# Column sums of the second weights moved from GpSimd to VectorE, from the fourth block on

## The chip, the cores and the metric

One core of a Trainium2 chip runs the kernel. TensorE (PE) multiplies matrices, VectorE (DVE) and ScalarE (ACT) work on elements, GpSimd (POOL) does a little of the same, and SyncE (SP) starts all transfers of data. Each engine runs its own queue in order and waits on semaphores where it needs another's result. The metric is the device time of one execution in microseconds (us).

## The reference, cut

Windowed attention over 4 batches, 8 heads, 576 positions, followed by two feed-forward layers on 2304 tokens:

```python
attn = softmax(where(0 <= i - j < 128, scale * q @ k.T - slope * |i - j|, -1e9)) @ v
x    = attn.transpose(0, 2, 1, 3).reshape(2304, 512)
h    = maximum(x @ w_in1, 0)
x    = (s * h * h + b) @ w_out1            # 512 -> 2048 -> 512
h    = maximum(x @ w_in2, 0)
out  = (h * h) @ w_out2
```

The first layer's `b` adds the same row to every token: `b` times the column sums of `w_out1`. The kernel adds that row afterwards, and so it needs those column sums.

## The kernel before

Every float32 number that TensorE multiplies is split into a high half and a low half in the format fp32r, and a product takes three matmuls (high by high, high by low, low by high). `split` makes the halves: ScalarE copies the high one (L99), VectorE subtracts to get the low one (L102). The weights come as 64-bit words and are made into float32 by `convert`, a chain over three engines for each part `st` of 128x1024 or 128x512: ScalarE L119, VectorE L120, ScalarE L121, VectorE L122, GpSimd L123 (an integer add), and then the split into `wih`/`wil` (first weights) or `woh`/`wol` (second weights). Layer 1 has four groups of weights (0 to 3); a group is 4 of the 16 slices of 128 hidden units.

The tokens go in blocks of 256 (`b`, `u`), nine in all with the one of tails. Attention of a block is made in four pairs of heads (`pair_unit`): scores `s` on PE, masked maximum on VectorE (L186), exponentials on ScalarE (L190), sums and reciprocals `nd` (L193, L194), scaling of the probabilities `pr` (L268), transposes `t` on PE (L270), output `u` on PE (L281), and the split of the output into `xh` and `xl`. In block (0, 1) the probabilities and their transposes lie in weight tiles that aren't needed yet and are named `f_`.

`mlp` runs the first layer over a block: for each slice `f` PE makes `ha` (12 matmuls, L357) in one of two PSUM buffers, ScalarE takes the ReLU and VectorE the square `ra` (L367, L368), the split gives `ga`, and two slices later PE multiplies `ga` with the second weights into `oa` (12 matmuls, L394). So a buffer of `ha` comes free with the `ra` of VectorE two slices on. The lambdas in `behind` (loads, conversions, attention pieces of later blocks, sums) are traced between the slices; a scheduler then orders each engine's queue by its own estimate of the times, with `issue_after` as an added edge of order on one engine.

The first three blocks are done in halves while the weights are still being converted (`half` over groups 0 and 1, `other` over groups 2 and 3, whose names are `hc`, `rc`, `gc`, `oc`). Blocks 3 to 6 then run over all slices, and behind them stand the tails' attention, the next blocks' attention and the column sums: `sum_rows` adds four slices' worth of `woh` and `wol`, 128x512 each, into `csum`, 32 additions in all. They are traced from block 3 on, but on GpSimd nothing holds them there: the scheduler puts them as early as their weights exist. `csum` is read once, by the matmuls of `sum_column` (L544) during the last block of layer 1.

Of the kernel before, what the change touches and what calls it, by code (L numbers as in the profile page):

```python
# [8 lines left out]
F32 = mybir.dt.float32  # L9
# [4 lines left out]
ALU = mybir.AluOpType  # L14
# [5 lines left out]
def attention_mlp2_kernel(ctx, tc, first0, first1, qkv0, qkv1, qkvt, w_in1, w_out1, s_in, b_in, w_in2, w_out2, out):  # L20
# [7 lines left out]
    nc = tc.nc  # L28
# [9 lines left out]
    BLK = 256  # L38
# [28 lines left out]
    csum = const.tile([P, DM], F32, tag="csum", name="csum")  # L67
# [23 lines left out]
    def split(hi, lo, src, copy, sub):  # L91
        copy(hi, src)
        sub(lo, src, hi.bitcast(F32))
# [4 lines left out]
    def act_copy(o, i):  # L98
        return nc.scalar.activation(o, i, AF.Copy)  # L99

    def dve_sub(o, a, b_):
        nc.vector.tensor_tensor(o, a, b_, ALU.subtract)  # L102


    n_g = [0]

    marks = []

    def convert(words, hi, lo):

        l32, h32 = words[..., 0], words[..., 1]
        with tc.issue_after(marks[-4]) if len(marks) > 3 else nullcontext():
            nc.scalar.activation(l32, l32.bitcast(U32), AF.Copy, scale=2.0 ** -29)  # L119
        nc.vector.scalar_tensor_tensor(l32, h32, -2 ** 31, l32, ALU.bitwise_and, ALU.bitwise_or)  # L120
        nc.scalar.activation(h32.bitcast(F32), h32.bitcast(F32), AF.Copy, scale=2.0 ** -112)  # L121
        nc.vector.tensor_scalar(h32, h32, 3, None, ALU.logical_shift_left)  # L122
        nc.gpsimd.tensor_tensor(l32, h32, l32, ALU.add)  # L123
        split(hi, lo, l32.bitcast(F32), act_copy, dve_sub)
# [73 lines left out]
    def pair_unit(b, u, hp):  # L198
# [3 lines left out]
        early = b == 0  # L202
# [5 lines left out]
        def probabilities():  # L208
# [25 lines left out]
            if early:  # L234
                passes = [(qr, kr)]
            else:
                nqk = BLK + nj * P
                qk = ap.tile([P, 2, BLK + 3 * P], F32R, tag="qk", name=f"qk{nm}", bufs=1)
                split(qk[:, 0, :nqk], qk[:, 1, :nqk], raw[:, :nqk], act_copy, dve_sub)
                (qh, kh), (ql, kl) = [(qk[:, y, :BLK], qk[:, y, BLK:nqk]) for y in range(2)]  # L240
                passes = [(qh, kh), (qh, kl), (ql, kh)]
# [13 lines left out]
        def outputs():  # L255
# [17 lines left out]
            up = ps.tile([P, 3 * P], F32, tag="u", name=f"u{nm}", bufs=1) if hp % 2 or u or not early else psum("o", f"u{nm}")  # L273

            with tc.issue_after(moved.ins):
                k = 0
                for i, (ka, ncol) in enumerate(tiles):
                    nk = ncol // P
                    for j in range(nk):
# [3 lines left out]
                                             skip_group_check=True)  # L283
                        k += 1
            xh, xl = xt[(b, u)]
            split(xh[:, hp, :], xl[:, hp, :], up[:, :BLK], act_copy if early and u else act_mark, dve_sub)
        return [probabilities, outputs]

    def first_pair(u, hp):
# [147 lines left out]
    wts1, wts2 = [], []  # L437
    pools = {"ps": ps}

    def psum(tag, name):  # L440
        return pools["ps"].tile([P, DM], F32, tag=tag, name=name)
# [56 lines left out]
    nc.sync.dma_start(b_sb, b_in.partition_broadcast(P))  # L498
    def sum_rows(g, j):

        for w in (wts1[g][2], wts1[g][3]):
            nc.gpsimd.tensor_tensor(csum, csum, w[:, j, :].bitcast(F32), ALU.add)

    nc.gpsimd.memset(csum, 0.0)
    sums = [lambda g=g, j=j: sum_rows(g, j) for g in range(NG) for j in range(GF)]
    tails = [[lambda b=b, hp=hp: tail_unit(b, hp) for hp in range(H // 2)] for b in range(B)]
    for i in range(NHALF, LAST - 1):
# [117 lines left out]
```

## Time and profile before

| | us |
|---|---|
| median of 3 runs | 1009.8 (1008.94 to 1010.32) |
| the profiled execution | 1010.16 |
| its span, first to last instruction | 1008.4 |
| PE busy | 974.3 (97%) |
| VectorE busy | 522.2 (52%) |
| ScalarE busy | 490.2 (49%) |
| GpSimd busy | 130.4 (13%) |
| the 32 additions on GpSimd, first start to last start | 38.0 to 167.1 |

A busy share is a mean over stages that differ: VectorE is nearly always at work in the first 170 us, in which weights are converted, and about half of the time after it. A busy PE is not PE at its peak, since its clock is granted in two levels, 1.2 and 2.4 GHz, shown as 0.5 and 1.0.

### The profile page before, as it was taken

The numbers are of one execution on the slowest core, as the hardware profiler recorded it, in microseconds if no ns is written. First come the engines' busy times: TensorE is split into PE (matmuls) and PEld (weight loads), VectorE is DVE, ScalarE is ACT, GpSimd is POOL, SyncE is SP. The second block draws the span as 40 slices with busy tenths as digits, with TensorE's granted clock in tenths as the row PEclk, the third lists the DMA queues.
The fourth block names the chain that finished last, engine by engine and source line by source line (L and its number), as shares of the span: only waits on it lengthen the run. The fifth ranks groups of instructions, "written<-read, shape, count | busy, mean of one in ns | idle before, by whom it ended". The sixth has DMA issues, their size and how long they took to land.

```text
span 1008.4 us, 16815 instructions
## 1 busy us (share of the span) xinstructions
PE 974.3 (97%) x6504; PEld 854.1 (85%) x6504; DVE 522.2 (52%) x1236; ACT 490.2 (49%) x1157; POOL 130.4 (13%) x118
## 2 busy tenths in 40 slices
PE   6899889999999999999999899999999999999997
PEld 4689778999989999899999888778888888898886
DVE  6997998443564444544265787754223222432222
ACT  7977766454555445554355666664222312322221
POOL 4653655000000000000010312310000000000000
PEclk9799989999999999999999999999999999999999
DMA  8135423111221211211052444422000100100001
GB/s 333 43 129 167 162 88 106 53 53 35 60 67 46 72 34 52 75 54 39 9 184 74 131 173 147 147 83 74 11 1 5 59 1 0 43 1 22 1 1 42
DMA packets 46928, 72.39 MB, mean 72 GB/s; under 512 B 6656, under 2 KB 27136, under 8 KB 46848
## 3 DMA queue, kind: packets, MB, share of 16 engines
q1 hardware_dynamic: 46848, 71.32, 21.8%
q8 instruction: 51, 0.84, 0.3%
q14 instruction: 29, 0.24, 0.1%
HBM read 59.77 MB, written 11.53 MB: 71 GB/s over the span
## 4 chain that ended last, share of the span: by engine, by line
PE 75%; DVE 9%; DMA 9%; ACT 4%; issue 2%; SPq 0%; POOL 0%; ACTq 0%; DVEq 0%; POOLq 0%
PE ob L403 15%; PE hb L357 14%; PE ha L357 13%; PE oa L394 13%; DMA st<-w_in 4%; PE oc L394 3%; PE s L245 3%; PE hc L357 3%; PE u L281 3%; DMA st<-w_out 2%; PE hbtail L357 2%; PE t L270 2%; PE obtail L403 2%; DVE wol L102 1%; DVE wil L102 1%
## 5 line engine op out<-in xcount | busy, mean ns | idle before, releaser
L394 PE MATMUL oa<-ga,woh 128*128 128x256 f32 x960 | 189.6, 289 | 7.3 <-ACT ga L99 3.9
L403 PE MATMUL ob<-woh,gb 128*128 128x512 f32 x512 | 168.9, 391 | 1.4 <-ACT gb L99 1.3
L394 PEld LDWEIGHTS oa<-ga,woh 128*128 128x128 f32 x960 | 152.2, 192 | 14.0 <-DVE ga L102 5.2
L394 PE MATMUL oa<-ga,wol 128*128 128x256 f32 x480 | 135.6, 286 | 0.1
L368 DVE SCALAR_TENSOR_TENSOR rb<-hb,rb 128x512 f32<-128x512 f32 x64 | 44.1, 690 | 147.4 <-ACT rb L367 147.2
L403 PEld LDWEIGHTS ob<-woh,gb 128*128 128x128 f32 x512 | 95.9, 188 | 23.8 <-ACT gb L99 3.3
L367 ACT ACTIVATE rb<-hb 128x512 f32<-128x512 f32 x64 | 38.2, 597 | 156.5 <-PE hb L357 152.0
L123 POOL TENSOR_TENSOR st<-st 128x512 int32<-128x512 int32 (+1 forms) x50 | 70.3, 1407 | 235.1 <-DVE st L122 177.4
L403 PE MATMUL ob<-wol,gb 128*128 128x512 f32 x256 | 99.7, 389 | 0.0
L394 PEld LDWEIGHTS oa<-ga,wol 128*128 128x128 f32 x480 | 92.2, 192 | 1.2 <-issue 0.9
L368 DVE SCALAR_TENSOR_TENSOR ra<-ha,ra 128x256 f32<-128x256 f32 x120 | 50.0, 419 | 62.9 <-ACT ra L367 62.4
L102 DVE TENSOR_TENSOR ga<-ra,ga 128x256 fp32r<-128x256 f32 x120 | 65.8, 552 | 29.0 <-ACT ga L99 28.4
L99 ACT ACTIVATE ga<-ra 128x256 fp32r<-128x256 f32 x120 | 49.5, 416 | 42.4 <-DVE ra L368 41.7
L102 DVE TENSOR_TENSOR gb<-rb,gb 128x512 fp32r<-128x512 f32 x64 | 45.5, 711 | 44.0 <-ACT gb L99 43.8
L367 ACT ACTIVATE ra<-ha 128x256 f32<-128x256 f32 x120 | 45.0, 378 | 43.6 <-PE ha L357 39.0
L99 ACT ACTIVATE gb<-rb 128x512 fp32r<-128x512 f32 x64 | 40.4, 632 | 47.7 <-DVE rb L368 35.6
L120 DVE SCALAR_TENSOR_TENSOR st<-st 128x512 int32<-128x512 int32 (+1 forms) x50 | 47.3, 950 | 26.3 <-ACT st L119 25.8
L119 ACT ACTIVATE st<-st 128x512 int32<-128x512 uint32 (+1 forms) x50 | 40.5, 814 | 35.2 <-DMA st<-w_out 19.3
L403 PEld LDWEIGHTS ob<-wol,gb 128*128 128x128 f32 x256 | 48.1, 188 | 9.7
L190 ACT ACTIVATE pr<-pr,nd 128x256 f32<-128x256 f32 (+1 forms) x96 | 45.1, 473 | 3.8 <-DVE nd L186 3.4
L121 ACT ACTIVATE st<-st 128x512 f32<-128x512 f32 (+1 forms) x50 | 40.5, 813 | 7.0 <-DVE st L120 7.0
L186 DVE CUSTOM_DVE_ANT_0 pr<-s,bases 128x256 f32<-128x256 f32 (+1 forms) x96 | 32.1, 386 | 19.4 <-PE t L270 15.0
(204 smaller groups left out, 2387.1 us busy)
## 6 DMA issues: line engine op xcount, KB each, us to landing
st<-w_out SPq DMA_DIRECT2D x20, 512.0 KB, 3.9
st<-w_in SPq DMA_DIRECT2D x8, 1024.0 KB, 6.8
st<-w_in SPq DMA_DIRECT2D x16, 512.0 KB, 4.8
st<-w_out SPq DMA_DIRECT2D x6, 1024.0 KB, 8.9
raw<-qkv SPq DMA_DIRECT2D x36, 128.0 KB, 2.6
xib<-acc SPq DMA_DIRECT2D x9, 512.0 KB, 4.4
out<-obb SPq DMA_DIRECT2D x16, 256.0 KB, 2.0
raw<-qkv SPq DMA_DIRECT2D x24, 160.0 KB, 2.9
```

What stands on the lines that cost most here:

```text
L99: return nc.scalar.activation(o, i, AF.Copy)
L102: nc.vector.tensor_tensor(o, a, b_, ALU.subtract)
L119: nc.scalar.activation(l32, l32.bitcast(U32), AF.Copy, scale=2.0 ** -29)
L120: nc.vector.scalar_tensor_tensor(l32, h32, -2 ** 31, l32, ALU.bitwise_and, ALU.bitwise_or)
L121: nc.scalar.activation(h32.bitcast(F32), h32.bitcast(F32), AF.Copy, scale=2.0 ** -112)
L123: nc.gpsimd.tensor_tensor(l32, h32, l32, ALU.add)
L190: nc.scalar.activation(pr, pr, AF.Exp, bias=nmx, scale=-1.0, accum_out=den)
L357: nc.tensor.matmul(ph, w_[:, cc, j * P:(j + 1) * P], x_[:, cc, :], start=(k == 0), stop=(k == 3 * NCC - 1))
L367: nc.scalar.activation(r, ph, AF.Relu)
L368: nc.vector.scalar_tensor_tensor(r, ph, 0.0, r, ALU.max, ALU.mult)
L394: nc.tensor.matmul(po[o // 2][:, (o % 2) * BLK:(o % 2 + 1) * BLK], w_[:, j, o * P:(o + 1) * P], g[:, gi, :], start=(start and n == 0 and o ...
L403: nc.tensor.matmul(po[t], g[:, gi, t * P:(t + 1) * P], w_[:, j, :], start=(start and n == 0), stop=(stop and n == 2))
```

## The change

`sum_rows` adds on VectorE instead of GpSimd, inside an `issue_after` on `lows[-1]`, the last low half of an attention output that was traced before it. `lows` is filled by `dve_mark`, which does what `dve_sub` does and keeps the instruction. Nothing else is edited; `csum` is still cleared by GpSimd.

```diff
+    def dve_mark(o, a, b_):
+        lows.append(nc.vector.tensor_tensor(o, a, b_, ALU.subtract).ins)
...
+    lows = []
...
-            split(xh[:, hp, :], xl[:, hp, :], up[:, :BLK], act_copy if early and u else act_mark, dve_sub)
+            split(xh[:, hp, :], xl[:, hp, :], up[:, :BLK], act_copy if early and u else act_mark, dve_mark)
...
     def sum_rows(g, j):
 
-        for w in (wts1[g][2], wts1[g][3]):
-            nc.gpsimd.tensor_tensor(csum, csum, w[:, j, :].bitcast(F32), ALU.add)
+        with tc.issue_after(lows[-1]):
+            for w in (wts1[g][2], wts1[g][3]):
+                nc.vector.tensor_tensor(csum, csum, w[:, j, :].bitcast(F32), ALU.add)
```

The diff adds four lines ahead of the kernel's body, so L102 of before is L102 (`dve_mark`) or L105 (`dve_sub`) of the change, L268 is L272, L368 is L372, and so on. Three places show what it moves.

GpSimd from the conversion of the last part of group 0 on, before; `st03` is part 3 of group 0, and `woh0`, `wol0` are the second weights of group 0:

```order
L123 TENSOR_TENSOR st03_326<-st03_326 128x1024
L502 TENSOR_TENSOR csum_90<-csum_90,woh0_317 128x512
L502 TENSOR_TENSOR csum_90<-csum_90,wol0_318 128x512
L123 TENSOR_TENSOR st10_337<-st10_337 128x1024
L502 TENSOR_TENSOR csum_90<-csum_90,woh0_317 128x512
L502 TENSOR_TENSOR csum_90<-csum_90,wol0_318 128x512
L502 TENSOR_TENSOR csum_90<-csum_90,woh0_317 128x512
L502 TENSOR_TENSOR csum_90<-csum_90,wol0_318 128x512
L123 TENSOR_TENSOR st11_480<-st11_480 128x1024
L502 TENSOR_TENSOR csum_90<-csum_90,woh0_317 128x512
```

The same place in the change:

```order
L127 TENSOR_TENSOR st03_326<-st03_326 128x1024
L127 TENSOR_TENSOR st10_337<-st10_337 128x1024
L127 TENSOR_TENSOR st11_480<-st11_480 128x1024
L127 TENSOR_TENSOR st12_676<-st12_676 128x1024
L127 TENSOR_TENSOR st13_718<-st13_718 128x1024
```

The sums that stood between two conversions, and ahead of the next one, are gone from this queue.

VectorE in block 3, around the low half of the fourth output of block (2, 0), before; `ra3_4` is the square of slice 4 of block 3, `pr0_t_2` a tail's probabilities:

```order
L102 TENSOR_TENSOR ga3_3_3047<-ra3_3_3048,ga3_3_3047 128x256
L316 TENSOR_SCALAR pr0_t_1_3075<-pr0_t_1_3075,nd0_t_1_3074 128x192
L102 TENSOR_TENSOR x2l_2086<-u2_0_3_2961,x2h_2085 128x256
L368 SCALAR_TENSOR_TENSOR ra3_4_3110<-ha3_4_3096,ra3_4_3110 128x256
L102 TENSOR_TENSOR ga3_4_3109<-ra3_4_3110,ga3_4_3109 128x256
L368 SCALAR_TENSOR_TENSOR ra3_5_3172<-ha3_5_3158,ra3_5_3172 128x256
L186 ISA pr0_t_2_3137,nd0_t_2_3136<-s0_t_2_3134,bases_97 64x192
```

The same place in the change:

```order
L105 TENSOR_TENSOR ga3_3_3047<-ra3_3_3048,ga3_3_3047 128x256
L102 TENSOR_TENSOR x2l_2086<-u2_0_3_2961,x2h_2085 128x256
L507 TENSOR_TENSOR csum_90<-csum_90,woh0_317 128x512
L507 TENSOR_TENSOR csum_90<-csum_90,wol0_318 128x512
L372 SCALAR_TENSOR_TENSOR ra3_4_3110<-ha3_4_3096,ra3_4_3110 128x256
L507 TENSOR_TENSOR csum_90<-csum_90,woh0_317 128x512
L105 TENSOR_TENSOR ga3_4_3109<-ra3_4_3110,ga3_4_3109 128x256
L507 TENSOR_TENSOR csum_90<-csum_90,wol0_318 128x512
L507 TENSOR_TENSOR csum_90<-csum_90,woh0_317 128x512
L190 ISA pr0_t_2_3137,nd0_t_2_3136<-s0_t_2_3134,bases_97 64x192
```

Five sums stand between that low half and the tail's scores, two of them ahead of `ra3_4` and three ahead of `ga3_4`; blocks 4 to 6 have much the same, with up to three ahead of the square and four ahead of its low half.

VectorE in block 0, around the first squares, before; `st10` and `st11` are the first two parts of group 1:

```order
L120 SCALAR_TENSOR_TENSOR st11_480<-st11_480 128x1024
L193 TENSOR_SCALAR nd0_1_2_553<-nd0_1_2_553 128x4
L194 RECIPROCAL nd0_1_2_553<-nd0_1_2_553 128x4
L368 SCALAR_TENSOR_TENSOR ra0_0_362<-ha0_0_348,ra0_0_362 128x256
L268 TENSOR_SCALAR f0_1_2woh_554<-f0_1_2woh_554,nd0_1_2_553 128x256 x2
L102 TENSOR_TENSOR wil1_340<-st10_337,wih1_339 128x4x256
L368 SCALAR_TENSOR_TENSOR ra0_1_429<-ha0_1_415,ra0_1_429 128x256
L122 TENSOR_SCALAR st11_480<-st11_480 128x1024
```

The same place in the change:

```order
L124 SCALAR_TENSOR_TENSOR st11_480<-st11_480 128x1024
L197 TENSOR_SCALAR nd0_1_2_553<-nd0_1_2_553 128x4
L198 RECIPROCAL nd0_1_2_553<-nd0_1_2_553 128x4
L272 TENSOR_SCALAR f0_1_2woh_554<-f0_1_2woh_554,nd0_1_2_553 128x256 x2
L105 TENSOR_TENSOR wil1_340<-st10_337,wih1_339 128x4x256
L372 SCALAR_TENSOR_TENSOR ra0_0_362<-ha0_0_348,ra0_0_362 128x256
L372 SCALAR_TENSOR_TENSOR ra0_1_429<-ha0_1_415,ra0_1_429 128x256
L126 TENSOR_SCALAR st11_480<-st11_480 128x1024
```

The low half of the first weights of group 1 has passed ahead of the first square `ra0_0`. PE at that place, before, from the last transposes ahead of slice 2:

```order
L357 MATMUL ha0_1_415<-x0l_126,wih0_256 128x256
L357 MATMUL ha0_1_415<-x0h_125,wil0_257 128x256
L270 MATMUL t0_1_01_396<-ident_75,f0_1_0wih_370 128x128 x4
L281 MATMUL u0_1_0_404<-f0_1_0wil_371,raw0_1_0_367 64x128 x4
L357 MATMUL ha0_2_482<-x0h_125,wih0_256 128x256
L357 MATMUL ha0_2_482<-x0l_126,wih0_256 128x256
L357 MATMUL ha0_2_482<-x0h_125,wil0_257 128x256
```

The same in the change:

```order
L361 MATMUL ha0_1_415<-x0l_126,wih0_256 128x256
L361 MATMUL ha0_1_415<-x0h_125,wil0_257 128x256
L274 MATMUL t0_1_01_396<-ident_75,f0_1_0wih_370 128x128 x4
L285 MATMUL u0_1_0_404<-f0_1_0wil_371,raw0_1_0_367 64x128 x8
L274 MATMUL t0_1_10_453<-ident_75,f0_1_0wih_370 128x128 x4
L361 MATMUL ha0_2_482<-x0h_125,wih0_256 128x256
L361 MATMUL ha0_2_482<-x0l_126,wih0_256 128x256
L361 MATMUL ha0_2_482<-x0h_125,wil0_257 128x256
```

Four matmuls of `u0_1_0` and four transposes, which followed slice 2, now stand ahead of it.

## Rows read from the trace of the kernel before

**Rows 1.** Windows: length, then PE, PEld, DVE, ACT, POOL busy; granted clock, DMA.

```profile
38.16:64.00 25.84, 22.17 (x166) 18.63 (x165) 25.07 (x44) 19.27 (x39) 18.00 (x11) 0.91 0.41 148
64.00:115.00 51.00, 48.76 (x414) 43.60 (x413) 43.96 (x103) 40.33 (x98) 21.97 (x13) 0.99 0.40 133
115.00:140.00 25.00, 19.94 (x136) 16.16 (x136) 24.15 (x35) 15.93 (x34) 16.70 (x11) 0.81 0.46 147
140.00:170.00 30.00, 28.63 (x229) 27.29 (x227) 25.17 (x46) 19.04 (x42) 18.10 (x13) 1.00 0.34 107
170.00:500.00 330.00, 330.00 (x2826) 303.81 (x2825) 157.40 (x571) 166.87 (x495) 2.44 (x16) 1.00 0.17 49
250.00:280.00 30.00, 30.00 (x264) 27.75 (x261) 15.72 (x62) 15.72 (x52) 0.61 (x4) 1.00 0.25 73
```

**Rows 2.** PE in time order, rows that waited: start, length, [wait, released by].

```profile
48.70 0.38 PE L357 MATMUL ha<-x0h,wih 128*128 128x256 f32 x1 [2.41 <-DVE ra L368]
...
121.96 0.39 PE L394 MATMUL oa<-ga,woh 128*128 128x256 f32 x1 [0.87 <-DVE ga L102]
...
127.06 0.50 PE L357 MATMUL ha<-x1h,wih 128*128 128x256 f32 x2 [0.77 <-ACT x1h L96]
...
130.13 0.41 PE L270 MATMUL t<-ident,pr 128*128 128x128 f32 x2 [1.65 <-DVE pr L268]
131.38 0.69 PE L270 MATMUL t<-ident,pr 128*128 128x128 f32 x2 [0.85 <-DVE pr L268]
...
164.19 0.39 PE L394 MATMUL oc<-gc,woh 128*128 128x256 f32 x1 [0.99 <-DVE gc L102]
```

**Rows 3.** The tile csum, half of its sums: min/median/max ns, first and last start.

```profile
L502 POOL TENSOR_TENSOR csum<-csum,woh x16: 1271/1456/2250, 38.0 to 165.4; 128x512 f32<-128x512 f32 x16
```

**Rows 4.** GpSimd in time order, one of four sums from 126 to 133 us.

```profile
129.91 1.27 POOL L502 TENSOR_TENSOR csum<-csum,woh 128x512 f32<-128x512 f32 x1
```

**Rows 5.** VectorE in time order, 125 to 133 us.

```profile
125.30 2.05 DVE L102 TENSOR_TENSOR wol<-st,woh 128x1024 fp32r<-128x1024 f32 x1 [0.17 <-ACT woh L99]
127.60 0.92 DVE L193 TENSOR_SCALAR nd<-nd 128x4 f32<-128x4 f32 x1
...
128.77 4.17 DVE L268 TENSOR_SCALAR pr<-pr,nd 128x256 f32<-128x256 f32 x4
```

**Rows 6.** VectorE's groups by form, 38 to 170 us: busy us, mean ns.

```profile
L102 DVE TENSOR_TENSOR ga<-ra,ga 128x256 fp32r<-128x256 f32 x24 | 23.2, 970 | 2.4 <-ACT ga L99 2.2
...
L268 DVE TENSOR_SCALAR pr<-pr,nd 128x256 f32<-128x256 f32 x16 | 7.7, 535 | 0.0
...
L193 DVE TENSOR_SCALAR nd<-nd 128x4 f32<-128x4 f32 x9 | 6.2, 683 | 2.3 <-ACT pr L190 2.3
```

**Rows 7.** The same view, 170 to 500 us.

```profile
L102 DVE TENSOR_TENSOR ga<-ra,ga 128x256 fp32r<-128x256 f32 x63 | 26.4, 424 | 20.5 <-ACT ga L99 20.4
...
L268 DVE TENSOR_SCALAR pr<-pr,nd 128x256 f32<-128x256 f32 x56 | 16.4, 348 | 0.2
...
L102 DVE TENSOR_TENSOR qk<-raw,qk 128x512 fp32r<-128x512 f32 x8 | 5.5, 686 | 1.5 <-ACT qk L99 1.5
...
L193 DVE TENSOR_SCALAR nd<-nd 128x4 f32<-128x4 f32 x18 | 3.1, 171 | 16.4 <-ACT pr L190 16.3
```

**Rows 8.** PE in time order after its long wait in block 0.

```profile
50.99 1.12 PE L281 MATMUL u<-f_0wil,raw 128*64 128x128 f32 x8
52.04 1.03 PE L270 MATMUL t<-ident,f_0wih 128*128 128x128 f32 x4
```

**Rows 9.** A window at the lower clock; columns as in rows 1.

```profile
131.40:138.10 6.70, 5.95 (x29) 4.89 (x30) 6.64 (x9) 4.59 (x8) 3.13 (x2) 0.50 0.14 54
```

**Rows 10.** Block 3 in time order: two rows of VectorE, then one of PE.

```profile
263.98 0.43 DVE L102 TENSOR_TENSOR x2l<-u,x2h 128x256 fp32r<-128x256 f32 x1 [2.31 <-ACT x2h L96]
...
267.29 0.43 DVE L102 TENSOR_TENSOR ga<-ra,ga 128x256 fp32r<-128x256 f32 x1 [2.26 <-ACT ga L99]
...
271.27 0.40 PE L394 MATMUL oa<-ga,woh 128*128 128x256 f32 x2
```

## The prediction

> **What bounds the kernel now.** I read the windows first [rows 1]. From 170 to 500 us PE is busy for all of 330 us at the full clock, while VectorE works for 157.4 us of them: there PE's own work sets the pace, and half of VectorE is free. Before 170 us it is the other way round. VectorE is busy 25.07 of 25.84 us, 43.96 of 51, 24.15 of 25 and 25.17 of 30, and PE stands idle for 3.67, 2.24, 5.06 and 1.37 us in the same four windows, with a mean granted clock of 0.91, 0.99, 0.81 and 1.00. Then I read who ends PE's waits there [rows 2]: `ra`, `ga`, `pr` and `gc`, all made by VectorE, and once `x1h` of ScalarE, which stands in the same chain.
>
> So VectorE bounds the first stage, and the next question is what it does. Its groups in 38 to 170 us [rows 6] are much slower than the same forms in 170 to 500 us [rows 7]: `ga` 970 ns against 424, `nd` 683 against 171, `pr` 535 against 348. A row of `nd` has four elements per partition; its work can't have grown. The two queues in time order show the cause: each scaling of `pr` in the 4.17 us from 128.77 us takes 1.04 us instead of 0.35 [rows 5], and GpSimd runs sums of 1.27 us over the same microseconds, one after the other [rows 4]. An instruction of VectorE that works from SBUF to SBUF waits for the sum that is running. And from 170 to 500 us, where the forms are fast, GpSimd works for only 2.44 us [rows 1].
>
> **What is removed.** 32 sums leave GpSimd [rows 3]. The 16 over high halves have a median of 1.456 us and the 16 over low halves do the same work, so they are about 32 x 1.456 = 46.6 us out of 18.00 + 21.97 + 16.70 + 18.10 = 74.8 us: some 60% of what GpSimd does from 38 to 170 us. The rest, the integer additions of the conversion, stays and goes on colliding.
>
> On VectorE the excess of the three groups is 24 x 0.546 = 13.1, 9 x 0.512 = 4.6 and 16 x 0.187 = 3.0 us [rows 6, 7], 20.7 us; at 60% about 12 us of it belong to the sums. The groups of the conversion itself are slowed as well (a `wol` of 2.05 us in [rows 5]), so 12 us is the low end for VectorE. What counts is how much of it PE gets, and that I take place by place.
>
> *Block 0, at 46 to 53 us.* PE waits 2.41 us for the square that frees a buffer of `ha` [rows 2]. In the trace that square stands behind an `nd` that a sum held up. But in the change `ra0_0` has also been passed by the low half of 128x1024, so I expect the square at about the same time as before. What is won is that four matmuls of `u` and four transposes stand ahead of slice 2 and run inside the wait: half of 1.12 and all of 1.03 us [rows 8], 1.6 us.
>
> *Blocks 1 and 2, at 115 to 140 us.* From 125.30 us VectorE needs 7.6 us for `wol`, `x1l`, `nd`, the reciprocal and four `pr` [rows 5]. Four `pr` at 0.348 are 1.4 us instead of 4.17, and `nd` 0.17 instead of 0.92 [rows 7]; the `wol` should fall toward the 1.2 us that the others of its size take, so the chain loses some 4.3 us. PE's waits inside it, 0.77 + 1.65 + 0.85 [rows 2], 3.3 us, are shorter than that and should go. The wait of 0.87 at 121.96 us comes with an integer addition that the sums had pushed back; I count 0.7. Right after these waits PE runs 6.70 us at half clock [rows 9], which costs 3.35 us. With PE kept at work there, I expect that drop to go too. Together 7.3 us.
>
> *Blocks 0 and 1 in `other`, at 140 to 170 us.* The wait of 0.99 us for `gc` [rows 2] stands behind a `wol` and beside the last sums: 1 us.
>
> Sum of the gains: 1.6 + 7.3 + 1.0 = 9.9 us. The bounds: nothing at all, if each wait is only taken over by the next engine, and all that the four windows lose, 3.67 + 2.24 + 5.06 + 1.37 = 12.3 us of idle PE and 25.84 x 0.09 + 51 x 0.01 + 25 x 0.19 = 7.6 us of clock, 19.9 us.
>
> **What is added.** 32 additions on VectorE, SBUF to SBUF, 128x512. The nearest row is `qk` at the same size and types, 686 ns [rows 7], so 32 x 0.686 = 22 us, eight in each of blocks 3 to 6, between 250 and 480 us. There VectorE is busy 15.72 of 30 us in the dense stretch [rows 1]; eight sums make it 21.2. The edge to the low half adds no wait of its own: the low half stands there anyway, and its semaphore wait is before (2.31 us of idle in block 3, [rows 10]). Queued behind the sums are the square and the low half of the slice, with 2 and 3 sums ahead in block 3, at most 3 and 4 later, 2.1 and 2.7 us. The low half of 267.29 us had waited 2.26 us for ScalarE and was used at 271.27 us, 3.5 us after its end [rows 10]. So most of the delay goes into VectorE's idle time and the rest into that slack. Bounds: 0, and 22 us if each sum ended in a wait of PE. It is nearest to the 0, by the slack; I take 1 us over the four blocks. SP's queue and the transfers keep their order but for a few that swap neighbours; I cost that at nothing, since the loads they stand with wait for tiles that the faster stage frees sooner. The sums are read behind block 7, and the last one stands at slice 6 of block 6; if it came late, `sum_column` would wait for its remainder. Clearing `csum` stays on GpSimd at the start, long done.
>
> So 1010.2 - 9.9 + 1 = 1001.3 us against the profiled execution's own time, which is 0.4 us above the median. I predict 1001 us.
>
> **A rule against it.** VectorE is all but full from 115 to 140 us [rows 1], and the change gives it 22 us more. Trainium skill, "Perfetto Trace Analysis", section "Optimizing Scalar/DVE Operations": where the vector engine is saturated, giving some of its work to GpSimd may make sense, though it warns that the two share a port to SBUF and that it might not help. By the first half alone the sums belong where they were, and a move would add up to 22 us; by the warning the trace of before is the case where it didn't help. The rows side with the warning: `nd` at 683 ns beside GpSimd's work and 171 without it.
>
> **The rivals.**
> *Nothing moves (1007.8 to 1011.8 us).* The first stage is a chain over three engines, and with VectorE sooner the next to be late could be ScalarE or a load: one of the waits [rows 2] is released by ScalarE already. Against it: in 115 to 140 us ScalarE is busy 15.93 of 25 us and the transfers 0.46 [rows 1]. It gives the gains of one place at most, less the cost: 1010.2 - 1.6 + 1 = 1009.6 us. Chance 0.12.
>
> *The sums hold PE (slower).* One mechanism: VectorE runs its queue in order, and the sums ahead of a square keep a buffer of `ha` shut. The place is slices 4 and 5 of blocks 3 to 6. It decides once the sums ahead of one low half exceed the 3.5 us of slack, five of them at 0.686; the order has up to four, and the tail's steps stand between them too. If six of the eight sums of each block were paid, 4 x 6 x 0.686 = 16.5 us, it would be 1010.2 - 9.9 + 16.5 = 1017 us. For it speaks that VectorE's idle time before 250 us lies in pieces; against it, PE had no wait in this whole stretch. Chance 0.12.
>
> *The drop of the clock stays.* The waits go, but PE's clock still falls near 131 us: 1001.3 + 3.4 = 1004.7 us. This is inside my forecast's own range of 995 to 1007.
>
> *All of it goes (990 to 995 us).* The idle time and the lower clock of the four windows vanish and the sums cost nothing: 1010.2 - 19.9 = 990.3 us. For it: the 12 us on VectorE leave out the conversion's own groups. Chance 0.10.
>
> **How the numbers follow.** The forecast with or without the drop of the clock has 0.66. Faster by over 0.2% (2 us, about what a measurement can tell from no change) is the forecast and the case above it, 0.76; within 0.2% is 0.12; slower is 0.12. The range of 8 in 10 runs from 991 us to 1009 us and leaves out the slower case and part of the one in which nothing moves.
>
> **What would show it.** In the profile after: `ga`, `nd` and `pr` in the first 170 us near 424, 171 and 348 ns, except beside an integer addition; PE's waits at 127 to 132 us gone; no window at half clock there, or one; the square of slice 0 in block 0 at about 48 us, as before. In blocks 3 to 6, sums of about 0.69 us and PE without rows that wait on `ra` or `ga`. The prediction is wrong if those forms stay slow without the sums, if the waits reappear under ScalarE or a transfer, or if PE waits in blocks 3 to 6.

## The result, and the profile after

The changed kernel takes 999.8 us (median of 4 runs, 998.7 to 1002.8) against 1009.5 us (4 runs, 1008.9 to 1010.3): ratio 0.9916, 95% interval 0.9900 to 0.9931. In a second comparison it took 1001.7 us against 1010.0, ratio 0.9910 (0.9893 to 0.9926). The prediction was 1001 us, so its total is right. Its sum is not: two of its terms are wrong by 4 to 5 us each, and that they cancel is luck.

To see where the time went I read three marks in the rows of PE in time order: the first matmul of `hc` (end of the three halves), the first `ha` of block 3 and the first `ha` of block 7. Rows of after; columns are start, length, engine, line, operation:

```profile
151.33 0.28 PE L361 MATMUL hc<-x0h,wih 128*128 128x256 f32 x1
...
244.97 0.38 PE L361 MATMUL ha<-x1h,wih 128*128 128x256 f32 x1
...
496.07 0.36 PE L361 MATMUL ha<-x3h,wih 128*128 128x256 f32 x1
```

In the first profile of before the same rows start at 156.47, 250.08 and 504.62 us. So the first stage gave 5.1 us (forecast 9.9). Blocks 3 to 6, where the sums now stand, take 251.10 us instead of 254.54: they gained 3.4 us where the forecast paid 1. The other 2.9 us between the two profiles come after block 7 has begun, where the order on PE is the same in both.

The windows of after (length; PE, PEld, VectorE, ScalarE, GpSimd busy; granted clock; DMA), to be held against [rows 1]; the last answers to the dense stretch there:

```profile
38.16:64.00 25.84, 23.43 (x172) 20.21 (x171) 22.40 (x45) 22.01 (x47) 5.68 (x3) 0.86 0.46 158
64.00:115.00 51.00, 49.09 (x424) 43.66 (x422) 38.72 (x103) 39.34 (x92) 8.60 (x4) 1.00 0.39 127
115.00:140.00 25.00, 20.59 (x144) 17.83 (x145) 19.29 (x38) 16.83 (x36) 7.29 (x4) 0.80 0.46 148
140.00:170.00 30.00, 29.54 (x247) 28.24 (x246) 21.75 (x56) 20.10 (x51) 4.22 (x4) 1.00 0.34 107
...
250.00:280.00 30.00, 30.00 (x265) 27.66 (x263) 21.68 (x68) 16.53 (x52) 0.30 (x2) 1.00 0.31 83
```

GpSimd falls from 74.8 to 25.8 us in the first four, and VectorE from 118.4 to 102.2 us. From 115 to 140 us VectorE is no longer full (19.29 us for 24.15), and yet PE is busy 20.59 us for 19.94 there, at a clock of 0.80 for 0.81: the window that was to give 7.3 us looks almost as before.

VectorE's groups of after, 38 to 170 us (busy us, mean ns), which answer to [rows 6], and the sums in their new place (min/median/max ns, first and last start), which answer to [rows 3]:

```profile
L105 DVE TENSOR_TENSOR ga<-ra,ga 128x256 fp32r<-128x256 f32 x24 | 14.4, 606 | 2.7 <-ACT ga L99 2.7
...
L272 DVE TENSOR_SCALAR pr<-pr,nd 128x256 f32<-128x256 f32 x16 | 4.7, 349 | 0.0
...
L197 DVE TENSOR_SCALAR nd<-nd 128x4 f32<-128x4 f32 x10 | 3.2, 321 | 3.0 <-ACT pr L194 2.6 <-ACT f_2woh L194 0.3
```

```profile
L507 DVE TENSOR_TENSOR csum<-csum,woh x16: 674/683/695, 250.4 to 460.7; 128x512 f32<-128x512 f32 x16
L507 DVE TENSOR_TENSOR csum<-csum,wol x16: 680/689/693, 252.3 to 461.4; 128x512 f32<-128x512 f32 x16
```

The slow forms fell as forecast: `pr` from 535 to 349, `nd` from 683 to 321, `ga` from 970 to 606 (what is left stands beside the integer additions). A sum costs VectorE 0.69 us, as taken from the row of `qk`.

PE's waits of after, in time order, block 0 and then 108 to 130 us, to be held against [rows 2]:

```profile
44.47 0.38 PE L361 MATMUL ha<-x0l,wih 128*128 128x256 f32 x1 [1.58 <-DVE x0l L102]
...
47.44 1.12 PE L285 MATMUL u<-f_0wil,raw 128*64 128x128 f32 x8 [0.75 <-ACT f_0wil L99]
...
120.95 0.66 PE L285 MATMUL u<-pt,raw 128*64 128x128 f32 x8 [0.81 <-ACT pt L99]
...
122.35 1.32 PE L249 MATMUL s<-qk 64*128 64x256 f32 x12 [0.75 <-DVE nd L190]
...
124.69 0.80 PE L361 MATMUL ha<-x1h,wih 128*128 128x256 f32 x2 [1.02 <-ACT x1h L96]
...
128.83 1.11 PE L274 MATMUL t<-ident,pr 128*128 128x128 f32 x4 [1.61 <-ACT pt L99]
```

The four waits from 120 to 130 us come to 4.19 us. The four of before in the same place, 0.87 + 0.77 + 1.65 + 0.85, were 4.14 us. They are as long as they were; only now ScalarE ends three of them. ScalarE's own rows, and one of VectorE, show what stands behind them:

```profile
116.12 0.38 ACT L99 ACTIVATE pt<-t 128x256 f32<-128x256 f32 x1
119.67 0.74 ACT L99 ACTIVATE qk<-raw 128x640 fp32r<-128x640 f32 x1 [3.18 <-DMA raw<-qkv]
120.31 0.58 ACT L99 ACTIVATE pt<-t 128x512 f32<-128x512 f32 x1
...
127.34 0.70 ACT L123 ACTIVATE st<-st 128x512 int32<-128x512 uint32 x1 [0.91 <-DMA st<-w_out]
```

```profile
120.44 0.83 DVE L105 TENSOR_TENSOR qk<-raw,qk 128x640 fp32r<-128x640 f32 x1 [2.54 <-ACT qk L99]
```

ScalarE runs its queue in order, and a copy that waits 3.18 us for the load of `raw` stands ahead of the `pt` for which PE waits at 120.95 us. The load is issued at 114.66 us and takes 4.35 us. VectorE waits 2.54 us for the same copy, and behind its row stand the masked maxima for which PE waits at 122.35 us; the exponentials that need them stand ahead of the `x1h` for which PE waits at 124.69 us. Ahead of the `pt` for which it waits at 128.83 us ScalarE waits another 0.91 us, for a load of `w_out`. This is read from the order of the rows; no run takes these loads away and leaves the rest alone.

The drop of the clock has only moved (0.50 is the lower level, 1.2 GHz):

```profile
45.60:52.40 6.80, 6.05 (x36) 5.32 (x35) 5.85 (x11) 5.17 (x12) 1.89 (x1) 0.50 0.39 127
...
124.10:134.30 10.20, 8.00 (x38) 6.94 (x38) 8.41 (x16) 7.96 (x17) 3.10 (x2) 0.50 0.51 177
```

Before had 3.4 us at half clock near 116 us and 6.8 us near 134 us [rows 9]; after has 10.2 us in one piece.

### The profile page after: what moved, and what is told of

It is laid out like the page before. It is cut to its first block, busy times and chain, and to the rows that moved or that the text cites. A ratio compares the mean times of both kernels' runs of the same rounds, so it can differ in the third digit from the quotient of the medians.

```text
span 996.9 us, 16799 instructions
## 1 busy us (share of the span) xinstructions
PE 968.4 (97%) x6504; PEld 852.6 (86%) x6504; DVE 519.4 (52%) x1268; ACT 489.5 (49%) x1157; POOL 80.6 (8%) x86
## 4 chain that ended last, share of the span: by engine, by line
PE 77%; DMA 8%; ACT 6%; DVE 6%; issue 2%; POOL 0%; SPq 0%; ACTq 0%; DVEq 0%; POOLq 0%
PE ob L407 15%; PE hb L361 14%; PE ha L361 14%; PE oa L398 13%; DMA st<-w_out 4%; PE oc L398 3%; PE s L249 3%; PE u L285 3%; PE hc L361 3%; DMA st<-w_in 3%; PE t L274 2%; PE hbtail L361 2%; PE obtail L407 2%; DMA xib<-acc 1%; DVE wil L105 1%
## 5 line engine op out<-in xcount | busy, mean ns | idle before, releaser
L372 DVE SCALAR_TENSOR_TENSOR rb<-hb,rb 128x512 f32<-128x512 f32 x64 | 44.1, 690 | 147.4 <-ACT rb L371 147.2
L372 DVE SCALAR_TENSOR_TENSOR ra<-ha,ra 128x256 f32<-128x256 f32 x120 | 50.1, 418 | 49.0 <-ACT ra L371 48.1
L105 DVE TENSOR_TENSOR ga<-ra,ga 128x256 fp32r<-128x256 f32 x120 | 57.1, 478 | 26.6 <-ACT ga L99 25.9
L105 DVE TENSOR_TENSOR gb<-rb,gb 128x512 fp32r<-128x512 f32 x64 | 45.5, 710 | 44.0 <-ACT gb L99 43.9
```

The source lines that it names most:

```text
L372: nc.vector.scalar_tensor_tensor(r, ph, 0.0, r, ALU.max, ALU.mult)
```

## The experiments

Theory 1: GpSimd's sums slow VectorE in the first stage, and their going is worth some 5 us there. Theory 2: blocks 3 to 6 gain because PE's new order mixes the kinds of matmul less often; the sums on VectorE cost nothing. Theory 3: what lies after 504 us differs between executions, not between the kernels. The rivals: all of the gain is the sums' going; or all of it is the new order; or the sums on VectorE do cost PE time.

All numbers together (us). "hc" is the start of the first `hc`, "3 to 6" the time from the first `ha` of block 3 to that of block 7, "rest" from there to the first `hb` of the second of the five passes over the second layer (the order on PE is the same in all kernels there). "Shapes" counts, in the trace, how often PE goes from a matmul on one shape of the array (128 x 128, 64 x 128 for `s`, 128 x 64 for `u`) to one on another, in 3 to 6.

| kernel | median | ratio to before (95%) | hc | 3 to 6 | shapes | rest |
|---|---|---|---|---|---|---|
| before, first profile | 1009.5 | | 156.47 | 254.54 | 148 | 185.61 |
| after, first profile | 999.8 | 0.9916 (0.9900-0.9931) | 151.33 | 251.10 | 132 | 182.70 |
| e1 no sums | 1003.4 | 0.9956 (0.9941-0.9971) | 151.30 | 254.54 | 148 | 183.59 |
| e2 both | 1005.3 | 0.9972 (0.9959-0.9984) | 156.26 | 251.00 | 132 | 184.41 |
| e3 GpSimd, late | 1005.8 | 0.9976 (0.9965-0.9987) | 149.95 | 256.64 | 148 | 185.72 |
| e4 320 columns | 1006.6 | 0.9987 (0.9975-0.9998) | 155.25 | 254.54 | 148 | 182.97 |
| e5 after again | 1001.7 | 0.9910 (0.9893-0.9926) | 150.77 | 251.53 | 132 | 182.84 |
| e6 before, low half first | 1003.9 | 0.9939 (0.9926-0.9952) | 153.96 | 250.96 | 130 | 183.05 |
| e7 after, low half first | 999.0 | 0.9896 (0.9880-0.9912) | 150.49 | 249.51 | 122 | 185.04 |
| e8 VectorE, early | 1005.8 | 0.9963 (0.9950-0.9976) | 153.85 | 254.54 | 148 | 183.86 |
| e9 before again | 1009.3 | 1.0005 (0.9991-1.0019) | 155.37 | 254.54 | 148 | 183.82 |
| e10 fourth raw, no sums | 1006.2 | 0.9967 (0.9955-0.9978) | 161.20 | 250.34 | 129 | 184.35 |
| e11 sums doubled | 1003.3 | 0.9946 (0.9932-0.9961) | 152.34 | 253.80 | 146 | 183.96 |
| e12 own block | 996.7 | 0.9872 (0.9855-0.9888) | 150.75 | 249.96 | 119 | 183.34 |

The kernel before had a median of 1007.8 us beside e1 to e4, 1010.0 beside e5 to e8 and 1009.2 beside e9 to e12, so across these groups the ratios compare and the medians don't. The columns "hc", "3 to 6", "shapes" and "rest" come from one profile in each row.

From the first `hc` to the first `ha` of block 3 it takes 93.5 to 94.3 us in twelve of the fourteen profiles, but 96.0 in e6 and 92.0 in e10. For these two `hc` alone does not say what the first stage gained.

**e1, no sums.** Of the change only the removal is left:

```diff
     def sum_rows(g, j):
-        with tc.issue_after(lows[-1]):
-            for w in (wts1[g][2], wts1[g][3]):
-                nc.vector.tensor_tensor(csum, csum, w[:, j, :].bitcast(F32), ALU.add)
+        return
```

> The changed kernel with no column sums at all: csum keeps its zeros, so the term b times the column sums is left out. TensorE's order is that of the changed kernel up to the end of the third block's half and of the second loads, and that of the kernel before from the fourth block on. Theory 1 (GpSimd's sums slow VectorE in the first stage, by a port the two share) and theory 2 (the fourth to sixth block gain because TensorE's new order there has fewer switches between kinds of matmul): the first hc matmul starts at 151.3 us as after the change (156.5 before), the fourth to seventh block take 254.5 us as before the change (250.1 to 504.6), not 251.1 as after it; whole time about 1004.4 us. Rival (the late blocks gain because something else of the sums' removal from GpSimd reaches them): 251.1 us there, 1001 us. Rival (the sums cost VectorE about 1 us, hidden in the reordering): under 250.5 us there, 999 us.

Measured: `hc` at 151.30 us and 254.54 us in blocks 3 to 6, both as theories 1 and 2 said. Without any sum the late blocks are slower than with 32 of them on VectorE.

**e2, both.** The change, and the old sums as well:

```diff
+    csum2 = ap.tile([P, DM], F32, tag="csum2", name="csum2", bufs=1)
+        for w in (wts1[g][2], wts1[g][3]):
+            nc.gpsimd.tensor_tensor(csum2, csum2, w[:, j, :].bitcast(F32), ALU.add)
```

> The changed kernel with the 32 sums of the kernel before added back on GpSimd, early, into a second tile that nothing reads. TensorE's order is that of the kernel before in the first stage and that of the changed kernel from the fourth block on. Theories 1 and 2: the first hc matmul starts at 156.5 us as before the change (151.3 after it), and the fourth to seventh block take 251.1 us as after it (254.5 before it): whole time about 1006 us. Rival (all of the gain comes from GpSimd's sums being gone): 1009.5 us, with 254.5 us in those blocks. Rival (the late blocks gain alone): under 1003 us.

Measured: 156.26 and 251.00 us. The two gains come apart. In the first stage e2 has PE's order of before as well as the sums, so e4 below has to tell these two apart. VectorE is as slow as before while GpSimd's sums run (38 to 170 us):

```profile
L105 DVE TENSOR_TENSOR ga<-ra,ga 128x256 fp32r<-128x256 f32 x24 | 23.2, 973 | 3.0 <-ACT ga L99 2.8
```

**e3, the sums late on GpSimd.**

```diff
-        nc.gpsimd.memset(pr[:, :Z], 0.0)
+        pmarks.append(nc.gpsimd.memset(pr[:, :Z], 0.0).ins)
...
-        with tc.issue_after(lows[-1]):
+        with tc.issue_after(pmarks[-1]):
             for w in (wts1[g][2], wts1[g][3]):
-                nc.vector.tensor_tensor(csum, csum, w[:, j, :].bitcast(F32), ALU.add)
+                nc.gpsimd.tensor_tensor(csum, csum, w[:, j, :].bitcast(F32), ALU.add)
```

> The sums stay on GpSimd but are ordered late, each behind the clearing of a tail's probabilities, which stands in the fourth to seventh block. TensorE's order is exactly that of the kernel without sums. Theory 1: the price of the sums on GpSimd is one of place: the first stage is as after the change (first hc matmul at 151.3 us), and in the late blocks, where VectorE is busy only half of the time, they cost TensorE 0 to 1 us on 254.5 us: whole time about 1004.4 to 1005.4 us. Rival (the collision is paid wherever the sums stand): the late blocks take 257 to 260 us, the whole 1007 to 1010 us.

Measured: 149.95 us for `hc`, and 256.64 us for the late blocks, 2.1 us more than with PE's same order in e1: between the two theories. It is paid once, in block 3, and the rows show how. VectorE, GpSimd and PE in time order:

```profile
247.11 3.72 DVE L273 TENSOR_SCALAR pr<-pr,nd 128x128 f32<-128x128 f32 x4
250.76 0.41 DVE L105 TENSOR_TENSOR ga<-ra,ga 128x256 fp32r<-128x256 f32 x1
```

```profile
246.63 1.28 POOL L514 TENSOR_TENSOR csum<-csum,wol 128x512 f32<-128x512 f32 x1
247.99 1.35 POOL L514 TENSOR_TENSOR csum<-csum,woh 128x512 f32<-128x512 f32 x1
249.42 1.26 POOL L514 TENSOR_TENSOR csum<-csum,wol 128x512 f32<-128x512 f32 x1
```

```profile
251.22 0.39 PE L402 MATMUL oa<-ga,woh 128*128 128x256 f32 x1 [1.46 <-DVE ga L105]
```

Four `pr` of 128x128, 0.28 us each elsewhere, take 0.93 us each beside three sums in a row; `ga` is queued behind them and PE waits 1.46 us. Blocks 4 to 6 take as long as in e1. (`hc` came 1.35 us earlier than in e1, with the same order on PE: executions, as e9 shows.)

**e4, 320 of 512 columns.**

```diff
-            nc.gpsimd.tensor_tensor(csum, csum, w[:, j, :].bitcast(F32), ALU.add)
+            nc.gpsimd.tensor_tensor(csum[:, :320], csum[:, :320], w[:, j, :320].bitcast(F32), ALU.add)
```

> The kernel before with each sum cut from 512 to 320 columns (the other 192 columns of the column sums are left out): the work of GpSimd's sums is five eighths, while TensorE's order in the first stage is nearly that of the changed kernel (118 of some 900 rows differ) and from the fourth block on that of the kernel before. Theory 1 (collision): five eighths of the 5.1 us stay, the first hc matmul starts at about 154.5 us, whole time 1007.6 us. Rival (the order on TensorE in the first stage is what gained): the first hc matmul starts at 151.3 us, whole time 1004.4 us.

Measured: `hc` at 155.25 us, with an order on PE close to that of after. So it is not the order that gained the 5 us. Five eighths of the sums' columns keep three quarters of the price or more (155.25 against 151.30 in e1 and 155.37 to 156.47 in before). In time on GpSimd they keep about as much, 35.8 of 48.5 us, since a sum of 320 columns takes more than five eighths of one of 512. `ga` stands between its two values:

```profile
L102 DVE TENSOR_TENSOR ga<-ra,ga 128x256 fp32r<-128x256 f32 x24 | 19.7, 825 | 1.6 <-ACT ga L99 1.6
```

**e5, after again.** No edit.

> The changed kernel once more, as a measure of what executions differ by. Theories 1 and 2: the first hc matmul at 151.3 us, 251.1 us for the fourth to seventh block, the same to 0.3 us; theory 3 (the stretch from the last block's eighth ha pair to the first hb matmul, 47.96 us in the changed kernel's profile and 50.29 in the kernel before, differs by execution and not by kernel): that stretch anywhere from 48 to 50.5 us, the whole time 999 to 1002 us. Rival to theory 3 (the change shortens it): 48 us again.

Measured: 150.77 us, 251.53 us in blocks 3 to 6 (0.6 us less and 0.4 more than in the first profile, both a little beyond what was allowed), and a rest of 182.84 us. The stretch of theory 3 took 48.5 us, which decides nothing.

**e6 and e7, the low half first.** One line, in before and in after:

```diff
-                passes = [(qh, kh), (qh, kl), (ql, kh)]
+                passes = [(ql, kh), (qh, kl), (qh, kh)]
```

> The kernel before, its sums on GpSimd early, with one line changed: the three passes of an attention's scores start with the low half of the queries, so that all twelve matmuls wait for the same subtraction and stand together. TensorE's order has 206 switches between kinds of matmul in the fourth to seventh block, where the kernel before has 228 and the changed one 214. Theory 2 (a switch saved is worth 3.44/14 = 0.25 us): those blocks take 254.5 - 5.4 = 249.1 us without any sum on VectorE. Rival (the gain there belongs to the sums on VectorE, not to the order): 254.5 us. The first stage is left out of this: its order changes too (156 switches for 165).

> The changed kernel with the same line: scores start with the low half of the queries. 207 switches in the fourth to seventh block for 214, 155 in the first stage for 162. Theory 2: those blocks take 251.1 - 1.7 = 249.4 us, the first stage is as after the change or up to 1.7 us shorter; the whole is 1.7 to 3.5 us below the changed kernel in the same comparison. Rival (order is worth nothing): the same time as the changed kernel.

Measured: 250.96 us for e6, with the sums on GpSimd and none on VectorE, and 249.51 us for e7. In the same comparison e7 has a median of 999.0 us and the changed kernel 1001.7, with intervals that overlap. So theory 2's core holds: the late blocks gain by the order alone. Its size did not hold for e6 (249.1 expected). PE's rows of one attention's scores, the third of block 3, in before, after and e6:

```profile
291.82 0.28 PE L357 MATMUL ha<-x1h,wih 128*128 128x256 f32 x1
292.03 0.38 PE L245 MATMUL s<-qk 64*128 64x256 f32 x1
292.34 0.39 PE L357 MATMUL ha<-x1l,wih 128*128 128x256 f32 x1
292.56 0.28 PE L357 MATMUL ha<-x1h,wil 128*128 128x256 f32 x1
...
293.13 0.38 PE L245 MATMUL s<-qk 64*128 64x256 f32 x1
...
294.70 0.73 PE L245 MATMUL s<-qk 64*128 64x256 f32 x7
...
296.54 0.50 PE L245 MATMUL s<-qk 64*128 64x256 f32 x3
```

```profile
285.62 0.38 PE L249 MATMUL s<-qk 64*128 64x256 f32 x2
...
286.61 0.86 PE L249 MATMUL s<-qk 64*128 64x256 f32 x10
```

```profile
292.59 0.97 PE L245 MATMUL s<-qk 64*128 64x256 f32 x12
```

The twelve matmuls stand in four groups, in two, in one. The 0.12 us from one `ha` to the next become 0.21 + 0.31 us where a single `s` stands between, while an `s` among others takes some 0.07. What costs is not the change of kind. I counted the changes of the array's shape in the traces afterwards: `t` runs on 128 x 128 like `ha` and `oa`, and a step between them costs nothing extra, while the steps to or from `s` or `u` take 0.17 to 0.26 us from start to start, each kind of step on average (31.6 us for 148 in before, 0.21 each), against 0.124 within 128 x 128. With 0.2 us for each change of shape saved, 254.54 - 0.2 x (148 - n), the line gives 251.3, 250.9 and 249.3 us for after, e6 and e7; measured are 251.1 (251.5 in e5), 251.0 and 249.5. The count was taken after these runs, so for them the line is a fit; e10 and e11 below were counted afterwards too, but did not set the 0.2.

The Trainium skill, "TensorEngine Tiling (Array Packing)", section "Key Properties", says that a change of tiling mode, unlike one of tile, drains TensorE. The longer steps in the traces fit that and give the price here, 0.2 us; that it is a drain the traces don't show.

**e8, the sums on VectorE, early.**

```diff
-        with tc.issue_after(lows[-1]):
-            for w in (wts1[g][2], wts1[g][3]):
-                nc.vector.tensor_tensor(csum, csum, w[:, j, :].bitcast(F32), ALU.add)
+        for w in (wts1[g][2], wts1[g][3]):
+            nc.vector.tensor_tensor(csum, csum, w[:, j, :].bitcast(F32), ALU.add)
```

> The changed kernel with the 32 sums on VectorE but not ordered behind anything: they run in the first stage, between the conversions (from about 50 us on), 32 x 0.69 = 22 us of VectorE there. From the fourth block on TensorE's order is that of the kernel before. Theory 1 (VectorE is what the first stage waits for, and what it loses to GpSimd's sums is of the size of the sums themselves): the collision goes and 22 us of VectorE's own work come, so that the first hc matmul starts anywhere from 153 to 158 us; the late blocks take 254.5 us; whole time 1006 to 1011 us. Rival (only the collision matters, VectorE has room): 151.3 us, whole time as without sums, 1003.4 us.

Measured: 153.85 us, between before and after, and 254.54 us. Its sums and its `ga` (38 to 170 us):

```profile
L506 DVE TENSOR_TENSOR csum<-csum,woh x16: 660/685/1850, 40.3 to 168.9; 128x512 f32<-128x512 f32 x16
```

```profile
L105 DVE TENSOR_TENSOR ga<-ra,ga 128x256 fp32r<-128x256 f32 x24 | 12.1, 514 | 0.0
```

32 sums of 0.69 us would be 22 us; some ran beside integer additions, and together they took 26.9 us of VectorE. They cost 2.6 us at `hc` against e1, while the same sums on GpSimd cost 4.1 to 5.2 us. So leaving GpSimd alone gives a part of the first stage's gain, and the late place the rest. How large each part is stays open: e8 has one profile and an order on PE of its own, executions with one and the same order on PE up to `hc` differ there by up to 1.4 us (e1 and e3, or after and e3), and by the ratios of the whole times e8 (0.9963) is hardly behind e1 (0.9956). VectorE was as busy as before, 117.4 us in the four windows for 118.4, and still `hc` came earlier, so its busy time alone doesn't set the pace.

**e9, before again.** No edit.

> The kernel before once more, for its profile. Theories 1 and 2: the first hc matmul at 156.5 us to 0.7 us, the fourth to seventh block at 254.5 us to 0.1 us. Theory 3 (what lies between the last block's eighth ha pair and the third of the second weights' groups differs by execution): 139.4 to 142.4 us from 548.0 to 690.2 us, as the ten profiles so far show for kernels whose program is the same there. Rival to theory 3 (the change shortens it): 142.2 us again, as in the first profile of this kernel.

Measured: 254.54 us to the hundredth. `hc` came at 155.37 us, 1.1 us earlier than in the first profile, beyond the 0.7 allowed. The stretch of theory 3 took 140.6 us instead of 142.2, the rest 183.82 instead of 185.61. Over the fourteen profiles the rest runs from 182.70 to 185.72 us and follows no edit (e3 and e7 are both above 185). So theory 3 holds at least in part: of the 2.9 us there in the first profiles, 1.0 is left between e5 and e9, less than kernels with the same program differ by. Both profiles of after were also the fastest of their runs.

**e10, a fourth buffer for raw.** It tests theory 4, that ScalarE's wait for `raw` is what holds PE between 108 and 140 us. It is the kernel without sums, with room made by a narrower `csum`:

```diff
-    NQKV, NPR, NPT = 3, 4, 2
+    NQKV, NPR, NPT = 4, 4, 2
...
-    csum = const.tile([P, DM], F32, tag="csum", name="csum")
+    csum = const.tile([P, P], F32, tag="csum", name="csum")
```

> The kernel without sums with a fourth buffer for the queries, keys and values (raw); to make room csum has 128 columns and all its matmuls read the same ones, so the column sums are left out here too. TensorE's order changes by it everywhere (202 switches in the fourth to seventh block for 228). Theory 4 (with the collision gone, the stretch from 108 to 140 us waits for ScalarE, whose queue stands some 3 us at 117 to 120 us behind a copy that waits for raw, whose load waits for a buffer): that wait falls below 0.5 us and the first hc matmul starts 1 to 3 us earlier than without sums, at 148.3 to 150.3 us. Rival (the transfers or VectorE take the wait's place): 151.3 us to 0.6 us. The late blocks by theory 2 at 0.16 us a switch, as two later kernels showed: 250.3 us.

Measured: `hc` at 161.20 us, 9.9 us later than in e1, while the late blocks (129 changes of shape) take 250.34 us; the line gives 250.7. ScalarE's wait for `raw` is gone, but the order on PE moved in hundreds of rows of the first stage. VectorE and PE in time order:

```profile
110.12 5.18 DVE L126 TENSOR_SCALAR st<-st 128x1024 int32<-128x1024 int32 x3
115.22 2.11 DVE L105 TENSOR_TENSOR ga<-ra,ga 128x256 fp32r<-128x256 f32 x1
```

```profile
117.38 0.58 PE L398 MATMUL oa<-ga,woh 128*128 128x256 f32 x1 [4.18 <-DVE ga L105]
```

Three shifts of the conversion now stand ahead of a `ga`, and PE waits 4.18 us. By the first `ha` of block 3 the kernel is 7.6 us behind e1, and the profiled execution, 1007.9 us, is one of the slower of its kernel (median 1006.2). The run doesn't tell what the wait for `raw` alone is worth: theory 4 is neither shown nor refuted.

**e11, twice the operations on VectorE.**

```diff
             for w in (wts1[g][2], wts1[g][3]):
                 nc.vector.tensor_tensor(csum, csum, w[:, j, :].bitcast(F32), ALU.add)
+            for w in (wts1[g][2], wts1[g][3]):
+                nc.vector.tensor_tensor(csum, csum, csum, ALU.max)
```

> The changed kernel with a second operation of the same size behind each sum on VectorE (the larger of csum and itself, which changes nothing): 64 operations of 0.69 us in the fourth to seventh block for 32, 44 us of VectorE for 22. The operations shift the order: 229 switches, where the kernel before has 228 and the changed one 214. Theory 2 (the sums' own time on VectorE is hidden in these blocks): 254.5 us to 0.5 us there. Rival (VectorE's time there costs TensorE some 1 us for each 22 us, as the prediction had it): 256.5 us or more.

Measured: 253.80 us, 0.2 us below the edge of what was expected; with 146 changes of shape the line gives 254.1. 44 us of VectorE in these blocks cost PE nothing.

**e12, an attention in its own block.** e7, and:

```diff
-zipped((pending + more[:5], 2), (sums[:4], 1)))
-        pending = more[5:]
+zipped((pending + more[:8], 2), (sums[:4], 1)))
+        pending = more[8:]
```

> The changed kernel with scores that start with the low half of the queries, and with all eight pieces of an attention in the block that begins it (8 for 5): 189 switches in the fourth to seventh block, where the version with 5 pieces has 207 and took 249.5 us. Theory 2 at 0.16 us a switch: 246.6 us there, and a whole some 3 us below that version, 995 to 997 us. Rival (the shorter spacing makes TensorE wait for the attention's other engines): 249.5 us or more, waits of TensorE over 0.4 us in these blocks, where there is one in the changed kernel.

Measured: 996.7 us (994.4 to 997.8), below both kernels; its interval lies below that of after (0.9893 to 0.9926 in e5). But blocks 3 to 6 took 249.96 us, not 246.6. It has 119 changes of shape, only 3 fewer than e7, for which the line gives 248.7, and waits have come, of which this row is the longest:

```profile
318.70 0.45 PE L329 MATMUL u_t<-pt_t,raw_t 128*64 128x64 f32 x8 [0.97 <-ACT pt_t L99]
```

So the total was met and the reason given for it was not: of the 2.4 us by which its median is below that of e7, measured in another comparison and with intervals that just overlap, its late blocks show none. That gain stays open.

## Why the prediction came out

**The bound: right.** VectorE's results are what PE waits for before 170 us, and the sums on GpSimd made VectorE slow. In the trace of before, the 24 `ga` take 1.27 us on average beside a sum (12 of them), 0.92 beside an integer addition (6) and 0.42 beside neither (6). e1, e4 and e2 move their mean from 605 over 825 to 973 ns with none, a part and all of the sums on GpSimd, and e3 does the same to `pr` in another place. The 4.17 us for four `pr` in [rows 5] are no 1.04 us each, as the prediction read them: three beside sums take 1.21 to 1.43 us, and the last, after them, 0.34.

A rival is that the sums held up the conversion in GpSimd's own queue. The rows speak against it: in before, 17 of the 18 integer additions up to 170 us start within 0.13 us of the end of the shift on VectorE that they wait for, and one 1.09 us after it; in after all 18 start within 0.13 us. The addition at 118.82 us, which the prediction had the sums push back, starts 0.08 us after its shift.

VectorE lost 16.2 us of busy time in the four windows, more than the 12 us that the prediction called the low end. The first stage was worth 4.9 us (two profiles of each kernel, `hc` at 155.9 and 151.05 us on average), half of the 9.9. It is clear of what executions differ by: e1 and e3 have PE's order of after and no sums on GpSimd there either, e2 has the order and the sums of before, and the four profiles of the one sort lie at 149.95 to 151.33 us, the three of the other at 155.37 to 156.47.

**Block 0, 1.6 us: right in size.** The square after the wait starts at 47.56 us (expected at about 48), and by the 121st `ha` matmul, at 85.76 us before, after is 2.0 us ahead. The marks between don't place it, since `ha` and `oa` alternate in another order there.

**115 to 140 us, 7.3 us: the step that failed.** From that matmul to the 241st `ha` (143.42 us before) after gains another 1.9 us. The sum for this place took each wait as gone because VectorE's chain shrank by more than the wait. That holds only if nothing else is late within the same microsecond. ScalarE was: its queue stood 3 us behind the load of `raw` in before too (3.06 us, ending at 122.02), out of sight beside VectorE's waits. This is the rival "nothing moves", which came true for this one place and not for the others, and it is one of the prediction's own signs of being wrong: the waits reappeared under ScalarE. That the load of `raw` is the cause is read from the rows, since e10 could not settle it. The 3.35 us for the clock were not gained either, as in the rival "the drop of the clock stays": half clock lasted 10.2 us from 110 to 140 us in before and in after, and 6.8 to 13.7 us from 110 to 144 us in all the others.

**140 to 170 us, 1.0 us: right.** 13.05 us from the 241st `ha` to the first `hc` became 11.85, and PE's wait for `gc` fell from 0.99 to 0.39 us, now ended by ScalarE.

**The sums' cost, 1 us: wrong in sign.** The slack that hid them was argued rightly: VectorE is busy 21.68 of 30 us where 21.2 were forecast, e11 shows that twice as many cost nothing either, and PE's waits of after from 244.8 to 496.2 us (total, times, longest) are this one:

```profile
PE pc L549 <- ACT xoa L99: 0.7, 1, 0.7
```

It is ended by an output of block 6 and not by a sum; before has the same wait of 0.7 us at 503.7 us.

What the sum lacked is a term for the order. The edge to the low half delays the attention's own steps on VectorE where the order is made, and with that the scores' matmuls come in fewer groups: 16 changes of shape fewer, 3.4 us. The order of the changed kernel is known before a run, so these changes could have been counted; the prediction looked in it only for what waits.

**The rival in which the sums hold PE** had its condition (five sums ahead of a low half) unmet, and e11, with twice the work in the same places and no further wait, speaks against its mechanism.

**The rule against it.** The Trainium skill, "Perfetto Trace Analysis", section "Optimizing Scalar/DVE Operations", weighs giving a saturated VectorE's work to GpSimd, with the warning that it might not help. e8 is that case measured: with the sums given to GpSimd (e9, `hc` at 155.37; 156.47 in the first profile) the first stage is 1.5 to 2.6 us slower than with the sums on the full VectorE. The warning decides here, by the sign; the size is as uncertain as said of e8.

So 1001 us was met by luck, because 5.0 us too much for the first stage stood against 4.4 us too little for blocks 3 to 6; the profile of after, 998.7 us, then lies 1 to 4 us below its kernel's other runs.

## What to carry to other kernels

Where a change moves the order on PE, count the changes of the array's shape in the stretches where PE is full, before predicting anything else: 0.2 us each here, and let the matmuls that need the operand that comes last come first, since then all of them can stand together; in blocks 3 to 6 that cost nothing. A wait that a faster engine removes is a gain only as far as no other queue stands still over the same microseconds, so look at every engine's queue inside the wait, also at those that are not named as its releaser. Elementwise work on GpSimd beside a full VectorE cost more than the same work on VectorE itself, though VectorE was full.

## What had not been expected of the hardware

A change of the array's shape costs some 0.2 us from start to start although no wait is recorded, and PE counts as busy meanwhile: in blocks 3 to 6 of before 31.6 of 254.5 us go by in steps from one shape to another.

The stretches at half clock in the first 60 us differ from one execution of the same program to the next. The window from 22 to 60 us, after (first profile, then e5):

```profile
22.00:60.00 38.00, 33.77 (x199) 25.39 (x196) 34.28 (x70) 34.92 (x72) 10.20 (x6) 0.73 0.34 121
```

```profile
22.00:60.00 38.00, 32.80 (x216) 24.65 (x215) 34.77 (x70) 35.39 (x73) 10.04 (x6) 0.87 0.37 127
```

The granted clock averages 0.73 and 0.87, and still the two stand only 0.6 us apart at the first `hc`: which suggests that PE waits there for other engines rather than for its own clock.
